# Recurrent scan gated by a SwiGLU block: B transposed on TensorE, C loaded turned last, token turns and stores on SyncE, all notices on GpSimd

## The chip, the cores and the metric

One core of one Trainium2 chip. The metric is the device time of one execution in microseconds (us); most executions of one kernel agree within about 1%, and medians are quoted with their lowest and highest. The profile is a trace of one execution.

## The reference

Cut to what matters: a layer norm, a complex diagonal recurrence over 2048 tokens, and a SwiGLU block whose output gates the result of the recurrence.

```python
# L = 2048 tokens, D = P = 448, F = 1792
xn = layernorm(x)
dt = exp(log_dt);  Lam_bar = exp(dt * Lam)
B_bar = ((Lam_bar - 1) / Lam)[:, None] * (B_re + 1j * B_im)
Bu = einsum("bld,pd->blp", xn, B_bar)
for t in range(L):                       # the scan
    h = Lam_bar * h + Bu[:, t, :]
y = 2 * einsum("blp,dp->bld", hseq, C_re + 1j * C_im).real + xn * Dskip
g = silu((silu(xn @ w_gate) * (xn @ w_up)) @ w_down)
out = x + y * g                          # bf16
```

## The kernel before

Tokens are worked in four quarters of 512. A *phase* `gu(q)` makes the gate and up products of quarter q: 14 blocks of 128 columns, two blocks to a *step*, so seven steps. `bu(q)` multiplies the tokens by B, `ssm_steps(q)` is the scan on VectorE, `down(q)` the third SwiGLU product, `out_sum(q)` the product with C. The order on TensorE is gu(0) with bu(0) inside, gu(1) with bu(1) inside, then down(0), bu(2), down(0), out_sum(0), gu(2), and so on; the tail is down(3) and out_sum(3).

D = 448 is three and a half blocks of 128. So each sum is split into two shares of half-height matmuls that run side by side, and in this program the second share of a bank starts only when the first has ended. Another engine passes that on: an empty instruction (`nop`) on that engine waits for the last matmul of the first share, and the second share waits for the `nop`. This is called a *notice*.

```python
    teller = [nc.gpsimd]

    def tell(mm):
        told = teller[0].nop(nofuse=True)            # the notice
        tc.add_manual_dep(told.ins, mm.ins.name, SYNC, reason="share")
        return told.ins.name

    def sums(banks, weights, q, c0, c1, between=None, told=None):
        for share, first in ((0, True), (1, False)):
            for n in range(len(banks)):
                ...                                  # the matmuls of this share
                        if not first and m == 0:
                            told_of(mm, left[n])     # second share waits for the notice
                if first:
                    left.append(tell(mm))
                    ...
            if first and teller[0] is nc.gpsimd:
                run_small(4)                         # four small GpSimd instructions
```

A queue of small GpSimd instructions (the parameters of the recurrence, 128x4 elements each) is emptied a few at a time *behind* each pair of notices. GpSimd works through its instructions in the order of the program, so a notice waits behind the small instructions put before it. After the fourth step of gu(0), the kernel before sends its notices on SyncE instead:

```python
    def tell_by_sync():
        teller[0] = nc.sync
        run_small(99)

    gu(0, bg, 2.0, {                     # what is issued after each step
        0: [on(table_sin, 0), on(table_phase, 2), on(table_sin, 1)],
        1: [on(b_clear), on(bu, 0, (0, 1), False), on(table_phase, 3), ...],
        2: [on(params_trig), on(bu, 0, (2,), True), *stats(6, 7), *sqrt(1)],
        3: [on(tell_by_sync), on(params_out), on(run_small, 99), *rstd_of(1),
            *norms(4, 5, 6, 7)],
        4: [on(c_weights, 0), *transposes(4, 5, 6, 7), on(ssm_steps, bg, 0)],
        ...
    }, begun)
```

SyncE also issues the loads, B and C turned (transposed by the DMA) among them; ScalarE issues the turns of the tokens and the stores of the output.

## Time and profile before

| | before |
|---|---|
| median of 3 runs | 201.40 us (201.29 to 201.56) |
| the profiled run | 204.13 us, span 202.3, mean clock 0.982 |
| first matmul of down(0) in that run | 74.55 us |
| third gate/up phase, gu(2), in that run | 97.11 to 120.59, 23.5 us |

The prediction shows the slices, TensorE's waits and the windows of the worst hole. The chain of waits: shares of the span by engine, followed back from the last instruction.

```profile
PE 46%; DVE 23%; SPq 11%; ACT 7%; DMA 7%; issue 3%; ACTq 1%; DVEq 0%
```

Only 46% of the chain runs over TensorE's own work although TensorE is busy for 92% of the span. Then GpSimd's timeline (start, duration, line, operation, out<-in with their sizes). The first line is from `params_fold`, the others are part of `params_out`:

```profile
15.60 0.32 POOL L315 TENSOR_SCALAR turn_m<-turn_m 128x12 f32<-128x12 f32 x1
...
30.06 0.49 POOL L315 TENSOR_SCALAR lam<-lam 128x4 f32<-128x4 f32 x1
30.64 0.21 POOL L315 TENSOR_TENSOR prod<-lam,pcol 128x8 f32<-128x8 f32 x1
30.93 0.20 POOL L315 TENSOR_TENSOR nb<-prod 128x4 f32<-128x4 f32 x1
```

Such a small GpSimd instruction takes 0.2 to 0.6 us in this trace, a power 1.0 to 1.1.

### The profile page before, as it was taken

What the parts mean: (1) busy time and instruction counts of PE and PEld (TensorE: products, weight loads), DVE (VectorE), ACT (ScalarE), POOL (GpSimd) and SP (SyncE); (2) the same over time, 40 slices, a digit from 0 to 9 for tenths busy, and PEclk for the clock granted to TensorE, in tenths of its full rate; (3) what the DMA queues carried; (4) which work ended last, traced back from release to release, by engine and by line L of the source; (5) the groups of instructions that cost most, each with busy time, mean ns of one, the idle gap of its engine ahead of it and who ended that gap; (6) DMA issues with size and microseconds to landing.
All of it is one profiled execution on the core that took longest, in us unless ns stands there. A gap on an engine that the chain in (4) does not pass through costs nothing.

```text
span 202.3 us, 3623 instructions
## 1 busy us (share of the span) xinstructions
PE 186.4 (92%) x1429; PEld 89.5 (44%) x1433; DVE 157.3 (78%) x243; ACT 102.7 (51%) x195; POOL 18.2 (9%) x42
## 2 busy tenths in 40 slices
PE   6786994999799999999989999999999999999990
PEld 2542431344344444455434554455444445555550
DVE  4859974097929999999989999997946889885063
ACT  2258794629798846451049755481267652402200
POOL 3374433000000200000003000000000000000000
PEclk9999999599999999999999999999999999999999
DMA  6755999990000022000110040000200000010011
GB/s 180 229 100 128 347 313 148 278 160 3 0 0 3 0 52 52 3 0 0 42 52 0 21 85 4 0 3 23 70 3 0 0 3 0 0 67 27 0 43 48
DMA packets 24648, 12.58 MB, mean 62 GB/s; under 512 B 14644, under 2 KB 24632, under 8 KB 24632
## 3 DMA queue, kind: packets, MB, share of 16 engines
q1 hardware_dynamic: 15248, 8.69, 17.5%
q10 hardware_dynamic: 9384, 3.68, 7.8%
q8 instruction: 11, 0.18, 0.3%
q14 instruction: 5, 0.04, 0.1%
HBM read 7.11 MB, written 1.84 MB: 44 GB/s over the span
## 4 chain that ended last, share of the span: by engine, by line
PE 46%; DVE 23%; SPq 11%; ACT 7%; DMA 7%; issue 3%; ACTq 1%; DVEq 0%
PE hd L563 16%; PE up L427 9%; SPq L158 9%; PE gp L427 9%; PE y L577 8%; DVE bu_im L500 3%; DMA Wu<-in_B_w_up_dram 3%; PE pb L427 3%; DVE tmp L494 3%; DVE bu_re L500 3%; DVE Vt L555 3%; DMA Wg<-in_B_w_gate_dram 2%; DVE C L390 2%; DVE ere L494 2%; ACT us L551 2%
## 5 line engine op out<-in xcount | busy, mean ns | idle before, releaser
L427 PE MATMUL up<-xT,Wu 64*128 64x512 bf16 (+1 forms) x406 | 89.0, 377 | 5.1 <-SPq L409 3.0
L427 PE MATMUL gp<-xT,Wg 64*128 64x512 bf16 (+1 forms) x406 | 90.3, 377 | 0.7 <-ACT xT L247 0.6
L550 ACT ACTIVATE gs<-gp 128x512 bf16<-128x512 f32 x56 | 34.1, 609 | 45.2 <-PE gp L427 17.6
L427 PEld LDWEIGHTS <-Wg 64*128 64x128 bf16 x406 | 37.5, 96 | 28.5 <-issue 6.3
L427 PEld LDWEIGHTS <-Wu 64*128 64x128 bf16 x406 | 37.6, 96 | 25.8 <-SPq L409 3.5
L563 PE MATMUL hd<-Wd,Vt 128*128 128x448 bf16 x224 | 43.4, 353 | 0.0
L551 ACT ACTIVATE us<-up 128x512 bf16<-128x512 f32 x56 | 34.4, 614 | 0.0
L563 PEld LDWEIGHTS <-Vt 128*128 128x128 bf16 x224 | 21.7, 98 | 21.3 <-issue 1.3
L555 DVE TENSOR_TENSOR Vt<-gs,us 128x2048 bf16<-128x2048 bf16 (+1 forms) x16 | 17.4, 1084 | 7.6 <-ACT us L551 7.6
L427 PE MATMUL pb<-xT,BT 64*128 64x512 bf16 x168 | 20.3, 376 | 3.2 <-DMA BT<-in_A_B_im_dram 1.6
L568 ACT ACTIVATE sg<-hd 128x448 bf16<-128x448 f32 x16 | 8.7, 545 | 28.2 <-PE hd L563 27.2
L590 DVE TENSOR_TENSOR t<-y,sg 128x448 f32<-128x448 f32 x16 | 10.0, 623 | 12.8 <-PE y L577 12.4
L577 PE MATMUL y<-C,H_re 128*128 128x448 bf16 x64 | 17.4, 352 | 0.0
L500 DVE TENSOR_TENSOR_SCAN bu_re<-rcol,H_re,ere 128x512 bf16<-128x512 f32 x12 | 15.1, 1268 | 0.0
L427 PEld LDWEIGHTS <-BT 64*128 64x128 bf16 x168 | 8.7, 94 | 13.9 <-issue 3.4
L225 POOL TENSOR_TENSOR sd<-vep,halves 128x1 bf16<-128x1 bf16 (+1 forms) x7 | 6.8, 970 | 84.0 <-DVE vep L220 78.3
L581 PE MATMUL y<-Dd,xT 128*128 128x128 bf16 x64 | 13.6, 212 | 0.0
L390 DVE SCALAR_TENSOR_TENSOR C<-nat,nb_im,c_tb 128x448 bf16<-128x448 bf16 (+1 forms) x4 | 2.7, 684 | 11.7 <-ACT c_tb L389 11.7
L577 PE MATMUL y<-C,H_im 128*128 128x448 bf16 x48 | 11.7, 353 | 0.0
L500 DVE TENSOR_TENSOR_SCAN bu_im<-rcol,H_im,eim 128x512 bf16<-128x512 f32 x9 | 11.4, 1261 | 0.0
L462 ACT ACTIVATE bu_re<-pb 128x512 bf16<-128x512 f32 x12 | 7.4, 614 | 7.6 <-PE pb L427 7.6
L218 DVE BATCH_NORM_STATS2 st<-x_all 128x6 f32<-128x448 bf16 x16 | 9.9, 617 | 1.6 <-DMA x_all<-in_A_x_dram 1.5
(87 smaller groups left out, 177.5 us busy)
## 6 DMA issues: line engine op xcount, KB each, us to landing
out_dram<-ob ACTq DMA_DIRECT2D x16, 112.0 KB, 1.7
Wd<-in_B_w_down_dram SPq DMA_DIRECT2D x1, 1568.0 KB, 7.6
x_all<-in_A_x_dram SPq DMA_DIRECT2D x3, 448.0 KB, 8.1
Wg<-in_B_w_gate_dram SPq DMA_DIRECT2D x3, 384.0 KB, 4.2
Wu<-in_B_w_up_dram SPq DMA_DIRECT2D x3, 384.0 KB, 5.6
Wg<-in_B_w_gate_dram SPq DMA_DIRECT2D x3, 128.0 KB, 3.4
Wu<-in_B_w_up_dram SPq DMA_DIRECT2D x3, 128.0 KB, 3.0
x_all<-in_A_x_dram SPq DMA_DIRECT2D x2, 112.0 KB
```

The costliest lines, as they stand in the source:

```text
L158: nc.sync.dma_start(out=dst[:, k, c0 : c0 + n], in_=cols, transpose=True)
L218: nc.vector.bn_stats(out=st[:], in_=x_all[:, n, :])
L427: mm = nc.tensor.matmul(banks[n][i][:, c0:c1], lhsT=weights[n][i][h, d, :], rhs=xT[h, d, q * W + c0 : q * W + c1], start=(first and m == 0 ...
L494: nc.vector.tensor_tensor(out=of(out, n), in0=of(a, n), in1=of(b, n), op=op)
L500: nc.vector.tensor_tensor_scan(out=T["b"][c][:, k, :], data0=rcol[:, k : k + 1].to_broadcast([P, W]), data1=T["e"][c][:, k, :], initial=in ...
L550: nc.scalar.activation(gs[:, i + j, :], gp_[:], ACT.Silu)
L551: nc.scalar.activation(us[:, i + j, :], up_[:], ACT.Copy)
L555: nc.vector.tensor_tensor(out=Vt[:, f0 : f0 + n, :], in0=gs[:, 0:n, :], in1=us[:, 0:n, :], op=ALU.mult)
L563: nc.tensor.matmul(hd, lhsT=Vt_of[q][:, fi, j * P : (j + 1) * P], rhs=Wd[:, fi, :], start=(fi == 0), stop=(fi == NF - 1),)
L577: nc.tensor.matmul(y, lhsT=h, rhs=C2[:, n, :], start=(n == 0), stop=(n == NS - 1))
L581: nc.tensor.matmul(y[:, s + c0 : s + P], lhsT=xT[:, n, m * P : (m + 1) * P], rhs=Dd[:, n, c0:P], start=False, stop=False,)
L590: nc.vector.tensor_tensor(out=t[:], in0=y, in1=sg[:], op=ALU.mult)
```

## The change

Its intent is to fill the holes of the first 55 us. B arrives as it lies in memory and is transposed on TensorE, beside loads that are still under way. The turned loads of C go to the end of the loads. The token turns and the output stores move from ScalarE to SyncE. Since SyncE is then busy, all notices go to GpSimd, whose small instructions now carry a cost label and are placed up to a sum of 2.0 behind each pair of notices; most carry 0.25, so that up to eight stand there instead of four. The work on C moves into gu(1), the parameters move later. The core of the diff:

```diff
-    load_turned(BT, A_B_re, 0, D)
-    load_turned(BT, A_B_im[KF * P : D, :], D, R)
-    load_turned(BT, A_B_im[0 : KF * P, :], KT * P, KF * P)
...
+    load_nat(0, A_B_re)
+    load_x(TQ, 2 * TQ)
     load_gu(C0, 768)
+    load_nat(1, A_B_im)
+    load_gu(768, F)
...
+    def b_transpose(c, d, eng):
+        tp = bank("tpb", BF16).rearrange("p (i w) -> p i w", i=2)
+        for i in range(2):
+            for k in (KF, *range(KF)):
+                ...
+                nc.tensor.transpose(tp[:, i, c0 : c0 + P], nat[:, c, k, blk(d + i)], Id[:])
+        ...                                   # one copy on ScalarE or VectorE
...
-        nc.scalar.dma_start(out=xT_of(n), in_=xn[n % TQ][:], transpose=True)
+        nc.sync.dma_start(out=xT_of(n), in_=xn[n % TQ][:], transpose=True)
...
-        told = teller[0].nop(nofuse=True)
+        told = nc.gpsimd.nop(nofuse=True)
...
-            if first and teller[0] is nc.gpsimd:
-                run_small(4)
+            if first:
+                run_small(2.0)
...
-        nc.scalar.dma_start(out=out2d[m * P : (m + 1) * P, :], in_=ob[:])
+        nc.sync.dma_start(out=out2d[m * P : (m + 1) * P, :], in_=ob[:])
...
     gu(0, bg, 2.0, {
...
+        0: [*stats(4, 5, 6, 7), *sqrt(1), on(table_phase, 0)],
+        1: [*bs(1), on(b_clear), *rstd_of(1), *norms(4, 5, 6, 7), on(table_sin, 0)],
+        2: [*transposes(4, 5, 6, 7), on(load_c), on(table_phase, 1), on(table_sin, 1),
+            on(bu, 0, (0, 1), False), on(table_phase, 2)],
+        3: [on(table_sin, 2), on(bu, 0, (2,), True), on(table_phase, 3)],
+        4: [on(table_sin, 3), on(params_trig)],
+        5: [on(params_out), on(ssm_steps, bg, 0)],
     }, begun)
```

More of the change, by code (lines that the diff above doesn't have):

```diff
@@ L134, with load_x, load_w @@
     two_pi = ctile([P, 1], F32, "two_pi")
-    def load_x(q):
+    def load_x(n0, n1):
         nc.sync.dma_start(
-            out=x_all[:, q * TQ : (q + 1) * TQ, :],
-            in_=x2d[q * W : (q + 1) * W, :].rearrange("(n p) d -> p n d", p=P),
+            out=x_all[:, n0:n1, :],
+            in_=x2d[n0 * P : n1 * P, :].rearrange("(n p) d -> p n d", p=P),
         )
-    def load_w(eng, dst, src, c0, c1):
+    def load_w(eng, eng2, dst, src, c0, c1):
         eng.dma_start(
@@ L147, in load_w, with load_nat, load_turned @@
         )
-        eng.dma_start(out=dst[:, KF, c0:c1], in_=src[blk(KF), c0:c1])
+        eng2.dma_start(out=dst[:, KF, c0:c1], in_=src[blk(KF), c0:c1])
     def load_gu(c0, c1):
-        load_w(nc.sync, Wg, B_w_gate, c0, c1)
-        load_w(nc.sync, Wu, B_w_up, c0, c1)
-    def load_turned(dst, src, c0, n):
-        for k in (slice(0, KF), slice(KF, KT)):
-            cols = src[:, 0 : KF * P] if k.start == 0 else src[:, blk(KF)]
-            nc.sync.dma_start(out=dst[:, k, c0 : c0 + n], in_=cols, transpose=True)
+        load_w(nc.sync, nc.sync, Wg, B_w_gate, c0, c1)
+        load_w(nc.sync, nc.sync, Wu, B_w_up, c0, c1)
+    def load_nat(i, src):
+        nc.sync.dma_start(
+            out=nat[:, i, 0:KF, :], in_=src[0 : KF * P, :].rearrange("(k p) f -> p k f", p=P)
+        )
+        nc.sync.dma_start(out=nat[:, i, KF, :], in_=src[blk(KF), :])
+    def load_turned(dst, src):
+        for k, cols in ((slice(0, KF), slice(0, KF * P)), (slice(KF, KT), blk(KF))):
+            nc.sync.dma_start(out=dst[:, k, :], in_=src[:, cols], transpose=True)
     nat = big.tile([P, 2, KT, D], BF16, name="nat", tag="vt")
+    natC = ctile([P, 2, KT, D], BF16, "natC")
     nc.vector.memset(Wd[:, 0, :], 0.0)
@@ L177 @@
         nc.sync.dma_start(out=x_all[:, n, :], in_=x2d[n * P : (n + 1) * P, :])
-    nc.sync.dma_start(
-        out=x_all[:, 2:TQ, :], in_=x2d[2 * P : W, :].rearrange("(n p) d -> p n d", p=P)
-    )
-    load_w(nc.scalar, Wu, B_w_up, 0, C0)
     for r, v in enumerate((A_log_dt, A_Lambda_re, A_Lambda_im, A_Dskip)):
         nc.scalar.dma_start(out=vrow[r : r + 1, :], in_=v.unsqueeze(0))
-    load_w(nc.sync, Wg, B_w_gate, 0, C0)
-    load_gu(C0, 768)
-    load_turned(BT, A_B_re, 0, D)
-    load_turned(BT, A_B_im[KF * P : D, :], D, R)
-    load_turned(BT, A_B_im[0 : KF * P, :], KT * P, KF * P)
-    load_x(1)
-    load_gu(768, 1280)
-    load_gu(1280, F)
-    load_x(2)
-    load_x(3)
-    load_turned(nat[:, 0], A_C_re, 0, D)
-    load_turned(nat[:, 1], A_C_im, 0, D)
+    load_w(nc.sync, nc.scalar, Wg, B_w_gate, 0, C0)
+    load_w(nc.sync, nc.scalar, Wu, B_w_up, 0, C0)
+    load_x(2, TQ)
+    load_nat(0, A_B_re)
+    load_x(TQ, 2 * TQ)
+    load_gu(C0, 768)
+    load_nat(1, A_B_im)
+    load_gu(768, F)
     nc.gpsimd.affine_select(
@@ L208, with gp, run_small @@
     )
+    small = deque()
+    def gp(fn, cost=0.25, **kw):
+        small.append((cost, lambda: fn(**kw)))
+    def run_small(budget):
+        while small and budget > 0:
+            cost, fn = small.popleft()
+            fn()
+            budget -= cost
     mv = ctile([P, NT, nc.vector.BN_AGGR_DIM], F32, "mv")
@@ L227, in ln_sqrt, with ln_sqrt_soon @@
         )
+    def ln_sqrt_soon(n0, n1):
+        small.appendleft((1.0, lambda: ln_sqrt(n0, n1)))
     def ln_rstd(n0, n1):
@@ L232, in ln_norm @@
     def ln_norm(n):
-        for out, cols in ((slice(0, KF * P), slice(0, KF * P)), (block(KF), blk(KF))):
+        parts = [(slice(0, D), slice(0, D))]
+        if n >= TQ:
+            parts = [(slice(0, KF * P), slice(0, KF * P)), (block(KF), blk(KF))]
+        for out, cols in parts:
             nc.vector.tensor_scalar(
@@ L244, in ln_transpose @@
         for k in range(KT):
-            nc.tensor.transpose(tp[:, k, :], xn[n % TQ][:, block(k)], Id[:])
+            nc.tensor.transpose(tp[:, k, :], xn[n][:, blk(k)], Id[:])
         if eng is nc.scalar:
@@ L278, in params_row @@
         return tv
-    def exp_of(out, in_):
-        nc.gpsimd.tensor_tensor(out=out, in0=euler[:], in1=in_, op=ALU.pow)
     def params_in():
+        g, tt = nc.gpsimd, nc.gpsimd.tensor_tensor
         are, aim = pcol[:, 0:KT, 1], pcol[:, 0:KT, 2]
-        exp_of(dtv[:], pcol[:, 0:KT, 0])
-        nc.gpsimd.tensor_tensor(out=zr[:], in0=dtv[:], in1=are, op=ALU.mult)
-        nc.gpsimd.tensor_tensor(out=zi[:], in0=dtv[:], in1=aim, op=ALU.mult)
+        gp(tt, 1.0, out=dtv[:], in0=euler[:], in1=pcol[:, 0:KT, 0], op=ALU.pow)
+        gp(tt, out=zi[:], in0=dtv[:], in1=aim, op=ALU.mult)
         for out, shift in ((thp[:], 0.0), (turn[:, 1, :], 0.25)):
-            nc.gpsimd.tensor_scalar(
-                out=out, in0=zi[:], scalar1=1.0 / (2.0 * math.pi), scalar2=shift,
-                op0=ALU.mult, op1=ALU.add,
-            )
-        exp_of(rcol[:], zr[:])
-    def fold(u, width):
-        a = work.tile([P, W], F32, name="a", tag="scr_a")[:, 0:width]
-        nc.vector.tensor_scalar(
-            out=a, in0=u, scalar1=ROUND, scalar2=ROUND, op0=ALU.add, op1=ALU.subtract
-        )
-        f = work.tile([P, W], F32, name="f", tag="scr_f")[:, 0:width]
-        nc.vector.tensor_tensor(out=f, in0=u, in1=a, op=ALU.subtract)
-        nc.vector.scalar_tensor_tensor(
-            out=a, in0=f, scalar=-1.0, in1=f, op0=ALU.mult, op1=ALU.max
-        )
-        return f, a
+            gp(g.tensor_scalar, out=out, in0=zi[:], scalar1=1.0 / (2.0 * math.pi),
+               scalar2=shift, op0=ALU.mult, op1=ALU.add)
+        gp(tt, out=zr[:], in0=dtv[:], in1=are, op=ALU.mult)
+        gp(tt, 1.0, out=rcol[:], in0=euler[:], in1=zr[:], op=ALU.pow)
     def cos_sin(c_out, s_out, f, a, sign):
@@ L309, in cos_sin @@
         nc.scalar.activation(c_out, a, ACT.Sin, scale=-TWO_PI, bias=half_pi[:])
-    small = deque()
-    def gp(fn, **kw):
-        small.append(lambda: fn(**kw))
-    def run_small(n):
-        while small and n:
-            small.popleft()()
-            n -= 1
     def wide(name):
@@ L343, in params_fold @@
         for k in range(KT):
-            gp(g.tensor_scalar, out=Dd[:, k, :], in0=Id[:], scalar1=pcol[:, k + k // KF, 3:4],
+            gp(g.tensor_scalar, 0.6, out=Dd[:, k, :], in0=Id[:], scalar1=pcol[:, k + k // KF, 3:4],
                scalar2=1.0, op0=ALU.mult, op1=ALU.mult)
@@ L370, in table_phase @@
     def table_phase(k):
-        u = work.tile([P, W], F32, name="u", bufs=1)
-        nc.vector.tensor_single_scalar(u[:], it_f[:], thp[:, k : k + 1], ALU.mult)
-        phase[k] = fold(u[:], W)
+        f = work.tile([P, W], F32, name="f", tag="scr_f")
+        a = work.tile([P, W], F32, name="a", tag="scr_a")
+        nc.vector.tensor_single_scalar(f[:], it_f[:], thp[:, k : k + 1], ALU.mult)
+        nc.vector.tensor_scalar(
+            out=a[:], in0=f[:], scalar1=ROUND, scalar2=ROUND, op0=ALU.add, op1=ALU.subtract
+        )
+        nc.vector.tensor_tensor(out=f[:], in0=f[:], in1=a[:], op=ALU.subtract)
+        nc.vector.scalar_tensor_tensor(
+            out=a[:], in0=f[:], scalar=-1.0, in1=f[:], op0=ALU.mult, op1=ALU.max
+        )
+        phase[k] = f[:], a[:]
     def table_sin(k):
         cos_sin(CT[:, k, :], ST[:, k, :], *phase.pop(k), two_pi[:] if k == KF else TWO_PI)
+    def b_transpose(c, d, eng):
+        tp = bank("tpb", BF16).rearrange("p (i w) -> p i w", i=2)
+        for i in range(2):
+            for k in (KF, *range(KF)):
+                c0 = blk(k).start if c == 0 else (k + 1) % KT * P
+                nc.tensor.transpose(
+                    tp[:, i, c0 : c0 + P], nat[:, c, k, blk(d + i)], Id[:]
+                )
+        tp = tp[:, :, c * R : c * R + D]
+        dst = BT[:, d : d + 2, c * D : (c + 1) * D]
+        if eng is nc.scalar:
+            nc.scalar.activation(dst, tp, ACT.Copy)
+        else:
+            nc.vector.tensor_copy(out=dst, in_=tp)
     def b_clear():
@@ L388, in c_weights @@
             tb = work.tile([P, W], F32, name="c_tb", tag="scr_" + "fa"[i])[h, 0:D]
-            nc.scalar.activation(tb, nat[h, 1, k, :], ACT.Copy, scale=v[h, k : k + 1])
+            nc.scalar.activation(tb, natC[h, 1, k, :], ACT.Copy, scale=v[h, k : k + 1])
             nc.vector.scalar_tensor_tensor(
-                out=C2[ho, o, :], in0=nat[h, 0, k, :], scalar=u[h, k : k + 1], in1=tb,
+                out=C2[ho, o, :], in0=natC[h, 0, k, :], scalar=u[h, k : k + 1], in1=tb,
                 op0=ALU.mult, op1=ALU.subtract,
@@ L403 @@
     SYNC = mybir.DependencyInfo(mybir.DependencyClass.Sync, mybir.DependencyReason.DATA)
-    teller = [nc.gpsimd]
     def tell(mm):
-        told = teller[0].nop(nofuse=True)
+        told = nc.gpsimd.nop(nofuse=True)
         tc.add_manual_dep(told.ins, mm.ins.name, SYNC, reason="share")
@@ L592, in finish @@
         nc.vector.tensor_tensor(out=ob[:], in0=t[:], in1=x_all[:, m, :], op=ALU.add)
-        nc.scalar.dma_start(out=out2d[m * P : (m + 1) * P, :], in_=ob[:])
+        nc.sync.dma_start(out=out2d[m * P : (m + 1) * P, :], in_=ob[:])
     bg = Background()
-    def tell_by_sync():
-        teller[0] = nc.sync
-        run_small(99)
     def on(fn, *args):
@@ L611 @@
         ln_transpose(n, nc.scalar)
-        warm(1 + 2 * n)
+        if n == 0:
+            warm(1)
+    nc.scalar.activation(pcol[:], params_row(), ACT.Copy)
+    warm(1)
     for n in range(2, TQ):
@@ L620 @@
         ln_norm(n)
-    ln_transpose(2, nc.scalar)
+    ln_transpose(2, nc.vector)
     ln_transpose(3, nc.vector)
-    nc.scalar.activation(pcol[:], params_row(), ACT.Copy)
     params_in()
     params_fold()
+    for d in range(0, KT, 2):
+        b_transpose(0, d, nc.scalar)
     gu_matmuls(0, 0, begun, W // 2, W)
     nc.sync.dma_start(out=Wd[:], in_=B_w_down.rearrange("(ft p) d -> p ft d", p=P))
-    table_phase(0)
-    table_phase(1)
+    load_x(2 * TQ, NT)
     bu_alloc(0)
@@ L641, in sqrt, with bs, load_c @@
     def sqrt(q):
-        return [on(ln_sqrt, q * TQ, (q + 1) * TQ)]
+        return [on(ln_sqrt_soon, q * TQ, (q + 1) * TQ)]
     def rstd_of(q):
         return [on(ln_rstd, q * TQ, (q + 1) * TQ)]
-    gu(0, bg, 2.0, {
-        0: [on(table_sin, 0), on(table_phase, 2), on(table_sin, 1)],
-        1: [on(b_clear), on(bu, 0, (0, 1), False), on(table_phase, 3), on(table_sin, 2),
-            on(table_sin, 3), *stats(4, 5)],
-        2: [on(params_trig), on(bu, 0, (2,), True), *stats(6, 7), *sqrt(1)],
-        3: [on(tell_by_sync), on(params_out), on(run_small, 99), *rstd_of(1),
-            *norms(4, 5, 6, 7)],
-        4: [on(c_weights, 0), *transposes(4, 5, 6, 7), on(ssm_steps, bg, 0)],
-        5: [on(c_weights, 1)],
-        6: [on(c_weights, 2)],
+    def bs(c):
+        return [on(b_transpose, c, d, nc.vector if d else nc.scalar) for d in range(0, KT, 2)]
+    def load_c():
+        load_turned(natC[:, 0], A_C_re)
+        load_turned(natC[:, 1], A_C_im)
+    gu(0, bg, 2.0, {
+        0: [*stats(4, 5, 6, 7), *sqrt(1), on(table_phase, 0)],
[5 more added lines that the diff above has]
+        5: [on(params_out), on(ssm_steps, bg, 0)],
     }, begun)
     bu_alloc(1)
-    gu(1, bg, 2.0, {
-        0: [on(bu, 1, (0, 1, 2), True), on(c_weights, 3)],
+    gu(1, bg, 1.7, {
+        0: [on(bu, 1, (0, 1, 2), True)],
         1: [*stats(8, 9), on(ssm_steps, bg, 1)],
-        2: stats(10, 11) + sqrt(2),
-        3: rstd_of(2) + norms(8, 9),
-        4: norms(10, 11),
-        5: transposes(8, 9),
-        6: transposes(10, 11),
+        2: [*stats(10, 11), *sqrt(2), on(run_small, 99), on(c_weights, 0)],
+        3: [*rstd_of(2), *norms(8, 9), on(c_weights, 1)],
+        4: [*norms(10, 11), *transposes(8, 9), on(c_weights, 2)],
+        5: [*transposes(10, 11), on(c_weights, 3)],
     })
@@ L688 @@
                 2: rstd_of(q + 3) + norms(n, n + 1),
-                3: norms(n + 2, n + 3),
-                4: transposes(n, n + 1),
-                5: transposes(n + 2, n + 3),
+                3: norms(n + 2, n + 3) + transposes(n, n + 1),
+                4: transposes(n + 2, n + 3),
             } if q + 3 < NQ else {})
```

## The prediction

> **What bounds the kernel now.** TensorE does. I read the 40 slices first, then TensorE's waits, then the windows and timelines around each wait.
>
> ```profile
> PE   6786994999799999999989999999999999999990
> DVE  4859974097929999999989999997946889885063
> ACT  2258794629798846451049755481267652402200
> PEclk9999999599999999999999999999999999999999
> ```
>
> A slice is 5.06 us. After slice 10 (about 55 us) TensorE is full nearly everywhere; what it loses lies in the first 55 us. The clock row has one 5, just after the slice with TensorE at 4. VectorE is empty in that slice and full from 60 us on, so it may become a rival. TensorE's waits name the holes:
>
> ```profile
> PE up L427 <- SPq L409: 3.0, 1, 3.0
> PE pb L427 <- DMA BT<-in_A_B_im_dram: 1.6, 1, 1.6
> PE pb L427 <- ACT gs L550: 1.4, 1, 1.4
> PE up L427 <- POOLq L409: 1.1, 2, 0.8
> PE up L427 <- DVE t L590: 0.8, 1, 0.8
> ```
>
> The largest is a notice: the second half of each sum waits for a semaphore that SyncE passes on (line 409). SyncE itself was held by the loads of C with transposition, as its timeline shows:
>
> ```profile
> 25.88 5.30 SPq L158 DMA_TRANSPOSE nat<-in_A_C_re_dram  x2
> 31.22 3.48 SPq L158 DMA_TRANSPOSE nat<-in_A_C_im_dram  x2
> 34.83 0.50 SPq L627 DMA_DIRECT2D Wd<-in_B_w_down_dram  x1
> ```
>
> The notice follows at 35.45, behind these three in SyncE's order. The windows give its second price: busy times of the five engines, then clock, DMA share and GB/s.
>
> ```profile
> 32.00:35.50 3.50, 0.49 (x8) 0.06 (x4) 1.23 (x1) 0.69 (x2) 0.21 (x2) 0.86 1.30 149
> 35.50:41.00 5.50, 5.50 (x28) 1.91 (x30) 1.03 (x2) 3.29 (x6) 0.00 (x0) 0.50 0.96 288
> ```
>
> For 5.5 us after the hole the granted clock is 0.50: 13 pairs of half-height matmuls start 0.425 us apart instead of 0.215, so 13 x 0.21 = 2.7 us more are lost. Last, ScalarE's timeline at the start of the third gate/up phase:
>
> ```profile
> 98.57 5.02 ACTq L593 DMA_DIRECT2D out_dram<-ob  x4
> 103.69 0.60 ACT L550 ACTIVATE gs<-gp 128x512 bf16<-128x512 f32 x1 [12.02 <-DVE ob L592]
> ```
>
> ScalarE stands 12 us behind its four stores, which wait for VectorE, while the PSUM banks of the gate/up step that ended near 100.1 us wait for it.
>
> **What the Trainium skill says.** "TensorE: Matmul & The Clock Gate", Part 1, has the array drop to half clock after an idle window of about 3.4 us and come back after a busy one. The trace agrees in kind: a hole of 3.0 us was enough, and half clock lasted 5.5 us. So filling that hole is worth nearly twice its length. The same page, Part 4, gives about 275 to 390 ns for one 128x128 transposition; here eight in a row took 0.83 us, 0.10 each, and I use that. "DMA: Bandwidth & Descriptors", Issuing engines are not separate DMA queues, says that another issuing engine saves only sequencer time. That is the point of the moved stores and turns: a turn holds its queue for about 1.25 us here, a plain transfer 0.35 to 0.5. "ScalarE: Activation LUTs", What ACT_TABLE_LOAD costs, gives 186 ns + 0.833 ns per element with immediate operands: 0.61 us for 512, where the trace has 0.60. I estimate the new 896-wide PSUM copies at 0.93 us from it.
>
> **The change, part by part.** I count on TensorE. A gate/up step of two blocks is 14 pairs x 0.215 = 3.0 us; a bu step of two blocks 3.0, of one block with the packed bank 2.4, of three with it 5.35.
>
> *Loads.* B arrives untransposed, so the turned loads that held SyncE from 7.8 to 17.6 us go. The built program shows every DMA waiting for the one eight places before it. By that rotation the last 64 rows of the first columns of Wg and Wu, now on ScalarE's queue, go out after the first Wu block and after the next ScalarE slot: about 5.3 and 5.8 us. Similar 64 KB pieces took 3.6 to 3.8 us to land, but there was more ahead of them, so I say 8.2 and 8.7. The first matmuls can start at about 7.4 (7.92 before; one norm instruction instead of two, ScalarE not stuck issuing), but the fourth row group waits until 8.7. The first half then ends at 9.9, against 9.45. Bytes ahead of Wu columns 256 to 768 are about 2.8 MB; at the 250 GB/s of the first microseconds from 2 us on they land near 13.1, just in time. Columns 768 on, another 2.6 MB with B_im, land near 23, needed at 24 to 27.
>
> *Transposes of B.* 32 at 0.083 to 0.10 us are about 3.0 us of new TensorE work, half before the second half of step 0, half after step 1. The copies, three on ScalarE and one on VectorE, lie beside it.
>
> *Timetable.* First half ends 9.9; tokens 2 and 3 turned, 10.7; B_re, 12.2; second half (1.5 us), 13.7 (before 13.4). Step 1, 16.7; B_im, 18.2; step 2, 21.2; bu(0), 24.2; step 3, 27.2; bu(0) rest, 29.6; steps 4 to 6, 38.6. Phase 1: step 0, 41.6; bu(1), 47.0; six steps, 65.0. In the trace of before phase 1 ended, and the first down matmul began, at 74.55. That is 9.6 us. Read as removed terms after 13.4 us: notices and issue gaps 0.9, B's DMA and gap 1.8, SyncE's notice 3.2, clock 2.7, bu(1)'s wait for ScalarE and its ragged restart 2.2, crumbs 0.2, sum 11.0; less B_im 1.5 and 0.3 at the start, 9.2. The two ways differ by 0.4; I take 9.3.
>
> *Notices on GpSimd.* A notice for the first block has 0.85 us to spare. The batches of small work cost up to 2.0 by their labels, but eight light operations such as copies and turn_m sum to about 3.2 us in the trace of before. One notice should come late by about 0.5 us: 8.8 left.
>
> *Stores on SyncE.* ScalarE can empty the banks of the third phase's first step at once. That phase took 23.4 us (97.1 to 120.5) against 21.0 of work. What stays is the second step waiting for y banks that VectorE frees late, about 0.8. Gain 1.6. The other phases and the tail (down, y, last store) don't change.
>
> Sum: 8.8 + 1.6 = 10.4; 201.4 - 10.4 = **191.0 us**.
>
> **Rivals.** *VectorE becomes the bound.* It is 95 to 98% busy from 60 to 140 us, and TensorE now arrives nine us earlier. For it: no slack in those slices, and the work on C (about 4.7 us) moves into the second phase. Against it: VectorE sits idle 6.7 us in 32 to 41 and 5.7 us in 41 to 60, and this is where the new order puts work. Placing its new order against my timetable, H of the first quarter is ready near 75.5 and wanted at 81; the first y is read 4.4 us late, against 5.0 before. If I am wrong by 3 us, the third phase waits longer: about 194.
>
> *The loads come late.* With 7.9 MB before the token turns in one queue, at 280 GB/s the turns land at 31 to 35 us and are wanted at 38.6. The step-1 weights have no margin. A hole of 1 to 3 us, and half clock if it nears 3 us, gives 193 to 197.
>
> *The wait was hidden anyway.* If SyncE's hole only handed over to another wait (tokens turned at 38.7 to 44.2 in before), half the gain stays: 196. Against it: after, the turns go out from about 19 us, not behind ScalarE's evictions.
>
> **Range and chances.** My sum 191.0; nothing lost at the start and no late notice makes it 188.5; one rival at its middle makes 194 to 195. Range 188 to 195.5. Only two rivals together, or a second half-clock stretch, bring it over 197.4: faster by over 2% 0.92, within 2% 0.07, slower 0.01.
>
> **What would show it.** Right: no clock dip near 35 us; no TensorE wait over 1 us between 14 and 60 us; no BT DMA in TensorE's waits; 32 new transposes of about 3 us in sum; the first down matmul near 65.5 us; ScalarE's 12 us wait before gs gone, and the third phase 22 us long. Wrong: a wait for Wg, Wu or xT DMA above 2 us, a clock of 0.5 after 10 us, GpSimd notices above 1.5 us in sum, or TensorE waiting for H or for y banks by more than 3 us.

## The result, and the profile after

| | before | after |
|---|---|---|
| median | 201.34 us, 4 runs (201.25 to 201.56) | 198.51 us, 4 runs (197.36 to 198.69) |
| ratio | | 0.9846 (95%: 0.9808 to 0.9884) |
| profiled run | 204.13 us, span 202.3, clock 0.982 | 198.54 us, span 196.8, clock 0.991 |
| first matmul of down(0) | 74.55 | 71.33 |
| gu(2) | 23.5 us | 21.7 us |

A ratio is the mean time of one kernel's fast runs over that of the other's of the same rounds, so it is not quite the ratio of the medians. 191.0 us had been predicted, with a range of 188 to 195.5. The slices after (40 of 4.92 us, tenths of busy time):

```profile
PE   7899799949999999999999999999999999999991
DVE  4698982499228999999899999998945799789263
POOL 3335940195002000000003000000000000000000
PEclk9999999996999999999999999999999999999999
```

After 55 us the rows look as hoped. But TensorE has a 4 again (39 to 44 us), with a clock of 6 in the next slice, and GpSimd, which had nothing to do at that time in the kernel before, shows a 9 in just that slice (and another at 20 to 25 us). TensorE's waits (engine, operation, line, what it waited for; sum in us, times, longest):

```profile
PE up L440 <- POOLq L422: 3.0, 1, 3.0
PE pb L440 <- POOLq L422: 1.3, 1, 1.3
PE warm L176 <- DVE Wd L167: 1.1, 1, 1.1
PE gp L440 <- DMA Wg<-in_B_w_gate_dram: 0.5, 1, 0.5
```

The waits for SyncE, for B's DMA, for ScalarE and for the output banks are gone. Two waits for notices on GpSimd (line 422) have come in, one of them 3.0 us long. (The wait for `Wd` is the start of the program, before and after alike.) The windows around it (busy time of TensorE, weight loads, VectorE, ScalarE, GpSimd with counts, then clock, DMA share, GB/s):

```profile
38.00:41.60 3.60, 3.56 (x34) 1.41 (x30) 3.57 (x5) 3.00 (x6) 2.62 (x4) 1.00 0.02 5
41.60:44.60 3.00, 0.01 (x2) 0.01 (x2) 2.97 (x4) 0.00 (x0) 2.84 (x4) 0.92 0.00 0
44.60:48.00 3.40, 3.40 (x20) 1.25 (x22) 3.37 (x5) 1.72 (x4) 2.56 (x3) 0.57 0.01 2
```

TensorE stands from 41.6 to 44.6 us, and for 3.4 us after that the clock averages 0.57, which costs another 3.4 x 0.43 = 1.5 us. No transfer is under way; VectorE and GpSimd are both busy for the whole hole. GpSimd's timeline shows what stands in front of the notice:

```profile
38.73 0.61 POOL L212 TENSOR_TENSOR lam<-lam,rcol 128x12 f32<-128x12 f32 x1 [11.77 <-PE up L440]
39.44 1.20 POOL L212 TENSOR_SCALAR lam<-lam 128x4 f32<-128x4 f32 x1
40.72 0.75 POOL L212 TENSOR_TENSOR prod<-lam,pcol 128x8 f32<-128x8 f32 x1
41.55 1.06 POOL L212 TENSOR_TENSOR nb<-prod 128x4 f32<-128x4 f32 x1
42.69 0.80 POOL L212 TENSOR_TENSOR prod<-lam,pcol 128x8 f32<-128x8 f32 x1
43.56 0.91 POOL L212 TENSOR_TENSOR nb<-prod 128x4 f32<-128x4 f32 x1
44.43 0.64 POOL L212 TENSOR_TENSOR b_re<-nb,rden 128x4 f32<-128x4 f32 x1
45.03 1.11 POOL L212 TENSOR_TENSOR b_im<-nb,rden 128x4 f32<-128x4 f32 x1
```

These are the instructions that took 0.2 to 0.5 us before. Now they take 0.6 to 1.2 us. VectorE's timeline of the same microseconds says why:

```profile
38.07 1.22 DVE L507 TENSOR_TENSOR tmp<-bu_im,ST 128x2048 bf16<-128x2048 bf16 x1
39.32 1.23 DVE L507 TENSOR_TENSOR ere<-ere,tmp 128x2048 bf16<-128x2048 bf16 x1
40.46 0.95 DVE L507 TENSOR_TENSOR eim<-bu_im,CT 128x1536 bf16<-128x1536 bf16 x1
41.33 1.23 DVE L568 TENSOR_TENSOR Vt<-gs,us 128x2048 bf16<-128x2048 bf16 x1
42.48 0.94 DVE L507 TENSOR_TENSOR tmp<-bu_re,ST 128x1536 bf16<-128x1536 bf16 x1
43.46 0.96 DVE L507 TENSOR_TENSOR eim<-eim,tmp 128x1536 bf16<-128x1536 bf16 x1
```

Read the two lists side by side. `ere` ends at 39.32 + 1.23 = 40.55, and GpSimd's `lam`, begun during it, at 40.64. `eim` ends at 41.41, `prod` at 41.47; `Vt` at 42.56, `nb` at 42.61; `tmp` at 43.42, `prod` at 43.49; `eim` at 44.42, `nb` at 44.47. Each small GpSimd instruction ends 0.05 to 0.1 us after the VectorE instruction that was running when it began, whatever its own size. Each of these six needs the result of the one before, so the next one begins just after VectorE has begun its next, and loses most of a VectorE instruction again. TensorE resumes at 44.59, after the `nb` that ended at 44.47.

Eight instructions stand in front of the notice, `b_re` and `b_im` too, and these two end only at 45.07 and 46.14. So this notice did not wait until everything before it had ended: it went once `b_im`, the last before it, had its input, that `nb`.

The Trainium skill has this. "SBUF — State Buffer", Who interferes with whom, says that "A DVE instruction with two SBUF inputs contends with a GpSimd instruction that reads SBUF", since VectorE's second input comes through the read port that the two engines share, and that the later of the two is blocked until the first has ended. All six VectorE instructions above take two SBUF inputs, and the trace agrees to within 0.1 us. The prediction does not name this page.

The second wait, 1.3 us before `pb` at 22.43, is of the same kind: on GpSimd's timeline

```profile
20.70 1.63 POOL L212 TENSOR_SCALAR turn_m<-turn_m 128x12 f32<-128x12 f32 x1
```

took 1.63 us where it took 0.32 before. It began beside a VectorE product (`Vt`, 20.68, 1.21 us) and ended at 22.33, just after VectorE's next instruction (`f<-it_f,thp`, 21.82, 0.47 us), so it seems to have lost two. The second of them has one tensor input and a column of scalars, so the sentence quoted does not cover it. TensorE resumes at 23.69, when the last small instruction in front of this notice (`den`, 23.66) has just begun.

What the change meant to do otherwise worked. The transposes of B on TensorE's timeline:

```profile
10.53 1.06 PE L383 MATMUL tpb<-Id,nat 128*128 128x128 bf16 x16
16.50 1.07 PE L383 MATMUL tpb<-Id,nat 128*128 128x128 bf16 x16
```

32 transposes took 2.13 us, against an estimate of 3.0.

### The profile page after: what moved, and what is told of

It reads as the page before. It is cut to its first block, busy times and chain, and to the rows that moved or that the text cites. A ratio compares the mean times of both kernels' runs of the same rounds, so it can differ in the third digit from the quotient of the medians.

```text
span 196.8 us, 3681 instructions
## 1 busy us (share of the span) xinstructions
PE 186.6 (95%) x1463; PEld 90.6 (46%) x1463; DVE 157.8 (80%) x241; ACT 104.9 (53%) x197; POOL 25.7 (13%) x42
## 4 chain that ended last, share of the span: by engine, by line
PE 88%; POOL 5%; DMA 3%; issue 1%; DVE 1%; SPq 1%; POOLq 0%; DVEq 0%
PE gp L440 23%; PE hd L576 22%; PE up L440 19%; PE y L590 11%; PE pb L440 9%; PE pk L463 2%; DMA Wg<-in_B_w_gate_dram 2%; PE y L594 2%; DMA Wu<-in_B_w_up_dram 2%; POOL turn_m L212 1%; POOL nb L212 1%; PE tpb L383 1%; POOL lam L212 1%; POOL prod L212 1%; POOL turn L212 0%
## 5 line engine op out<-in xcount | busy, mean ns | idle before, releaser
L440 PE MATMUL up<-xT,Wu 64*128 64x512 bf16 (+1 forms) x406 | 87.4, 373 | 3.0 <-POOLq L422 3.0
L440 PE MATMUL gp<-xT,Wg 64*128 64x512 bf16 (+1 forms) x406 | 88.4, 373 | 0.5 <-DMA Wg<-in_B_w_gate_dram 0.5
L440 PEld LDWEIGHTS <-Wu 64*128 64x128 bf16 x406 | 36.9, 95 | 24.0 <-POOLq L422 4.0
L576 PEld LDWEIGHTS <-Vt 128*128 128x128 bf16 x224 | 21.7, 98 | 21.3 <-issue 1.3
L440 PE MATMUL pb<-xT,BT 64*128 64x512 bf16 x168 | 19.5, 379 | 1.3 <-POOLq L422 1.3
L590 PE MATMUL y<-C,H_re 128*128 128x448 bf16 x64 | 17.4, 352 | 0.0
L440 PEld LDWEIGHTS <-BT 64*128 64x128 bf16 x168 | 8.0, 95 | 12.4 <-issue 2.0
L590 PE MATMUL y<-C,H_im 128*128 128x448 bf16 x48 | 11.7, 353 | 0.0
L605 DVE TENSOR_TENSOR ob<-t,x_all 128x448 bf16<-128x448 f32 x16 | 10.0, 624 | 0.6
```

Source lines behind the costliest of these rows:

```text
L440: mm = nc.tensor.matmul(banks[n][i][:, c0:c1], lhsT=weights[n][i][h, d, :], rhs=xT[h, d, q * W + c0 : q * W + c1], start=(first and m == 0 ...
L576: nc.tensor.matmul(hd, lhsT=Vt_of[q][:, fi, j * P : (j + 1) * P], rhs=Wd[:, fi, :], start=(fi == 0), stop=(fi == NF - 1),)
L590: nc.tensor.matmul(y, lhsT=h, rhs=C2[:, n, :], start=(n == 0), stop=(n == NS - 1))
L605: nc.vector.tensor_tensor(out=ob[:], in0=t[:], in1=x_all[:, m, :], op=ALU.add)
```

## The experiments

Twelve runs were made, two of them of the unchanged kernels, on three chips, and each is compared with runs of the kernel before on its own chip. The theory: *VectorE's two-input products stretch the small GpSimd instructions, and the notice behind them is late.* Rivals: the start or the clock is at fault; SyncE or the loads; the number or order of the GpSimd instructions as such; the wait merely uncovers another one.

### Notices by SyncE over the critical stretch

```diff
+    teller = [nc.gpsimd]
-        told = nc.gpsimd.nop(nofuse=True)
+        told = teller[0].nop(nofuse=True)
...
-        5: [on(params_out), on(ssm_steps, bg, 0)],
+        5: [on(params_out), on(tell_by, nc.sync), on(ssm_steps, bg, 0)],
...
-        1: [*stats(8, 9), on(ssm_steps, bg, 1)],
+        1: [on(tell_by, nc.gpsimd), *stats(8, 9), on(ssm_steps, bg, 1)],
```

> The changed kernel, with the notices given by SyncE instead of GpSimd for the last gate/up step of phase 0, the first of phase 1 and bu(1) only; nothing else moves. Theory A (a notice stands behind eight small GpSimd instructions that are stretched beside VectorE's bf16 work): the hole of 3.0 us near 41.6 us and the half clock after it go, the small instructions stay slow (lam to nb_im about 8 us in sum), time 198.5 - 3.0 - 1.2 = 194.3 us. Theory B (TensorE would have waited there for PSUM banks or for ScalarE anyhow): a hole of 2 to 3 us stays, with another releaser, time 197.5 to 198.5.

Measured: 194.84 us (193.90 to 195.21, 4 runs), ratio 0.9647 (0.9582 to 0.9712). The 3.0 us hole and the low clock behind it are gone, and the first matmul of down(0) moves from 71.33 to 67.89 us, although this profile has a low clock (0.50 from 8.7 to 12.0 us) that the one of the kernel after does not have. The small instructions are as slow as in the kernel after:

```profile
39.50 1.08 POOL L212 TENSOR_SCALAR lam<-lam 128x4 f32<-128x4 f32 x1
40.67 1.14 POOL L212 TENSOR_TENSOR prod<-lam,pcol 128x8 f32<-128x8 f32 x1
```

So it is not their slowness as such that costs, but that a notice stands behind them. Taking the notice out of that queue brings most of the loss back. The 1.3 us wait before `pb`, where the notices stayed on GpSimd, is still there.

### The parameters one step earlier

```diff
-        3: [on(table_sin, 2), on(bu, 0, (2,), True), on(table_phase, 3)],
-        4: [on(table_sin, 3), on(params_trig)],
-        5: [on(params_out), on(ssm_steps, bg, 0)],
+        3: [on(table_sin, 2), on(bu, 0, (2,), True), on(table_phase, 3), on(params_trig)],
+        4: [on(table_sin, 3), on(params_out)],
+        5: [on(ssm_steps, bg, 0)],
```

> The changed kernel, with the sine of the parameters one step earlier and the nine small GpSimd instructions that follow it one step earlier, in 33 to 37 us, where VectorE stands idle; same instructions, same number, notices still by GpSimd. Theory A (VectorE's work stretches them): the nine take about 2.5 to 3.5 us instead of 8, the hole is below 0.7 us, time about 194.5 us. Theory C (it is only their number and order before the notice): the hole stays near 3 us, merely a step earlier, time 198 us.

Measured: 194.43 us, the median of the three fast runs (194.10 to 195.47; 194.95 with the slow one), ratio 0.9654 (0.9587 to 0.9721, fast runs). The profiled run, 197.09 us, was slow in its first 15 us and is not used for times; its timelines of GpSimd,

```profile
39.46 0.21 POOL L212 TENSOR_TENSOR prod<-lam,pcol 128x8 f32<-128x8 f32 x1
39.74 0.20 POOL L212 TENSOR_TENSOR nb<-prod 128x4 f32<-128x4 f32 x1
40.02 0.20 POOL L212 TENSOR_TENSOR prod<-lam,pcol 128x8 f32<-128x8 f32 x1
40.30 1.14 POOL L212 TENSOR_TENSOR nb<-prod 128x4 f32<-128x4 f32 x1
```

and of VectorE

```profile
40.15 1.23 DVE L507 TENSOR_TENSOR ere<-bu_re,CT 128x2048 bf16<-128x2048 bf16 x1 [6.13 <-ACT CT L310]
```

show the switch: the same instruction, `nb`, takes 0.20 us while VectorE is idle and 1.14 us once `ere` has begun. The number and order of the GpSimd instructions are those of the kernel after, so number and order alone are refuted.

### The scan one step later

```diff
-        5: [on(params_out), on(ssm_steps, bg, 0)],
+        5: [on(params_out)],
...
-        0: [on(bu, 1, (0, 1, 2), True)],
+        0: [on(bu, 1, (0, 1, 2), True), on(ssm_steps, bg, 0)],
```

> The changed kernel, with VectorE's scan work of the first quarter begun one step later and GpSimd left as it is: the other way round to keep the two apart. Theory A: the nine small instructions take 3 to 4 us, only the Vt product of VectorE lying beside them, the hole is below 1 us; VectorE gets 4 us later, which may cost up to 2 us at the first y banks: 194.5 to 196.5 us. Theory C: hole stays 3 us, 198 to 200 us.

Measured: 197.20 us (196.26 to 198.53), ratio 0.9785 (0.9717 to 0.9853), not resolved against 2%, and above the 194.5 to 196.5 expected. Nothing about GpSimd was edited, yet

```profile
38.77 0.21 POOL L212 TENSOR_TENSOR lam<-lam,rcol 128x12 f32<-128x12 f32 x1 [11.76 <-PE up L440]
39.07 1.27 POOL L212 TENSOR_SCALAR lam<-lam 128x4 f32<-128x4 f32 x1
40.43 0.20 POOL L212 TENSOR_TENSOR prod<-lam,pcol 128x8 f32<-128x8 f32 x1
```

of the six from the first `lam` to the second `nb` all are short but the one that began beside the only VectorE product there (`Vt`, 39.02 to 40.25). The last three, from 41.43 on, lie beside VectorE's next instructions and take 0.69 to 1.18 us; `b_im` ends at 43.26, and TensorE works through from 41 to 44 us all the same. The hole is gone and down(0) begins at 66.89 us. But VectorE is now late with the last quarter's scan, and TensorE waits for it at 181.8 us:

```profile
PE y L590 <- DVE H_re L507: 2.2, 1, 2.2
```

So the mechanism is confirmed from the other side, and VectorE's slack at the end is shown to be small: this order of work gives back 2.2 us of what it gains.

### The kernel before with its notices on GpSimd

```diff
-        3: [on(tell_by_sync), on(params_out), on(run_small, 99), *rstd_of(1),
+        3: [on(params_out), on(run_small, 99), *rstd_of(1),
...
-        1: [*stats(8, 9), on(ssm_steps, bg, 1)],
+        1: [on(tell_by_sync), *stats(8, 9), on(ssm_steps, bg, 1)],
```

> The kernel before, with one part of the change: the notices stay on GpSimd until the second step of phase 1, so that none stands behind SyncE's turned loads of C. If SyncE's order alone made the 3.0 us hole of the kernel before (my prediction's first term), it goes and the time falls by 3 us, to 198.3; if ScalarE's scaling of C, which needs the same loads, takes its place (rival: the wait was hidden anyhow), ScalarE stops at c_tb until about 38.5 us, TensorE stops for PSUM banks a step later, and the time is 200 to 201.5.

Measured: 201.74 us (201.29 to 202.91), ratio 1.0014 (0.9954 to 1.0074). The SyncE wait is gone, and in its place stands

```profile
PE gp L427 <- DMA xT<-xn: 4.3, 1, 4.3
```

TensorE waits for the turned tokens of the next quarter until 43.74 us. ScalarE issues their four turns from 35.57 to 41.39 us here and from 35.74 to 41.42 in the usual run of the kernel before (shown in the section "The kernel before, once more"), so the earlier notice did not bring them forward. That run stands twice, 1.7 us for SyncE and 2.2 us until 43.54; this one stands once, 4.3 us, and ends the wait at the same time. So in the kernel before the notices alone are worth nothing that these runs can measure: a second wait stood behind. That ScalarE's place as issuer held the turns back is argued; no run moved the turns alone. The expectation named another second wait, for ScalarE's scaling of C; it did not come.

### The kernel after again, and with four more warm-up matmuls

The first is the unchanged kernel, for comparison. The second adds fillers while the first weights arrive:

```diff
         if n == 0:
-            warm(1)
+            warm(2)
     nc.scalar.activation(pcol[:], params_row(), ACT.Copy)
-    warm(1)
+    warm(4)
```

> The changed kernel unchanged, on the chip and in the rounds of the three that follow, to compare them with. Expected 198.3 us, 197.3 where the profile shows no stretch of half clock; hole of 3.0 us near 41.6 us.

> The changed kernel with four more filler matmuls before its first gate/up step (2 and 4 instead of 1 and 1), where TensorE otherwise waits for the last rows of Wg and Wu until about 8.4 us. Two profiles of the last call showed half clock between 8 and 15 us, costing up to 2.8 us. Theory A [...]: no half clock before 20 us in the profile, time 0.3 to 1 us below the changed kernel's, with less spread. Theory B (the early half clock has another cause, or is rare): same time within 0.3 us.

Measured: 199.66 us (198.53 to 200.47), ratio 0.9848 (0.9771 to 0.9925), and 199.38 us (198.92 to 200.56), ratio 0.9847 (0.9775 to 0.9919). The same holes, 3.0 and 1.3 us, and the same low clock behind the first stand in the repeat. The fillers made no difference. Neither of these two profiles has a low clock in its first 15 us, so whether they protect a run that has one stays open.

### Stores by ScalarE again

```diff
-        nc.sync.dma_start(out=out2d[m * P : (m + 1) * P, :], in_=ob[:])
+        nc.scalar.dma_start(out=out2d[m * P : (m + 1) * P, :], in_=ob[:])
```

> The changed kernel with its 16 stores issued by ScalarE again. Theory (my prediction's 1.6 us): ScalarE waits about 12 us behind its stores at the start of phase 2, the third gate/up phase takes 23.4 us instead of 21.7, time 1.6 us above the changed kernel's, 199.9. Rival (VectorE's late release of the y banks sets that phase's start anyhow): under 0.5 us of difference.

Measured: 200.01 us (199.09 to 200.74), ratio 0.9881 (0.9802 to 0.9960), so 0.35 us over the repeat by medians, with ranges that overlap. ScalarE again stands behind its stores,

```profile
94.77 4.60 ACTq L606 DMA_DIRECT2D out_dram<-ob  x4
99.42 0.60 ACT L563 ACTIVATE gs<-gp 128x512 bf16<-128x512 f32 x1 [10.73 <-PE up L440]
```

but TensorE has no hole there, and gu(2) takes 21.8 us, as long as with the stores on SyncE (21.7). So the move of the stores is not what shortened gu(2) from 23.5 us. What differs from before is when VectorE is through: it reads the first output bank at 93.1 us in the kernel after, before gu(2) begins at 93.7, against 97.3 for a phase that begins at 97.1 in the kernel before. TensorE's waits say the same: in gu(2) of the kernel before it waits 0.8 us for VectorE's `t` (`PE up L427 <- DVE t L590` in the prediction's list), the instruction that reads an output bank, and in the kernel after that wait is gone. An earlier VectorE as the cause fits these times and was not tested by itself.

### B turned by the DMA, the rest of the change kept

```diff
-    load_nat(0, A_B_re)          # natural load + 16 TensorE transposes
+    load_bt(0)                   # turned load straight into BT
-    load_nat(1, A_B_im)
+    load_bt(1)
-    for d in range(0, KT, 2):
-        b_transpose(0, d, nc.scalar)
```

(names shortened; the B_im transposes go too.)

> The changed kernel with B loaded turned by DMA again, at the places where it now loads B untransposed; the 32 transposes on TensorE and their copies go. Theory A (turned loads hold SyncE about 1.25 us each and delay all weights behind them): TensorE saves 2.1 us of transposes and waits 3 to 5 us more for Wg, Wu or BT in its first 25 us, time 199.5 to 202. Theory B (queue room was enough, and B on TensorE costs its 2.1 us for nothing): about 196.3.

Measured: 199.00 us (197.49 to 200.29), ratio 0.9817 (0.9730 to 0.9904), which is not resolved from the repeat's 0.9848. My theory, that B's turned loads would hold up the weights by 3 to 5 us, is wrong: no wait for B stands in TensorE's list. But the rival's 196.3, the whole 2.1 us saved, did not come either. This run's profile has six waits of 0.2 to 0.7 us, 2.3 us together, in its first 14 us, where the kernel after has one of 0.5 (the start, `Wd`, left out in both); it also has a low clock from 8.5 to 18.5 us, so its times say little. The TensorE transposes cost 2.1 us and bring nothing that these runs can measure.

### Three versions put together

The first has the earlier parameters, the fillers, and half the room for small GpSimd instructions behind each pair of notices between step 2 and the last sine of gu(0):

```diff
-                run_small(2.0)
+                run_small(room[0])       # 2.0, but 1.0 from step 2 to table_sin(3)
```

The second is the first with B turned by the DMA. The third is the first with the last sine, the parameters and the first scan another step earlier:

```diff
-        3: [on(table_sin, 2), on(bu, 0, (2,), True), on(table_phase, 3), on(params_trig)],
-        4: [on(table_sin, 3), on(set_room, 2.0), on(params_out)],
-        5: [on(ssm_steps, bg, 0)],
+        3: [on(table_sin, 2), on(bu, 0, (2,), True), on(table_phase, 3), on(table_sin, 3),
+            on(set_room, 2.0), on(params_out)],
+        4: [on(ssm_steps, bg, 0)],
```

with `params_trig` moved to the end of step 2.

> e2_trig_early, with the batch of small GpSimd work after one sum halved between the second gate/up step and the sine of the parameters (four light instructions instead of eight ahead of the next notice), and the extra fillers of w_warm. Theory A: the 1.3 us hole near 22 us goes as well, TensorE waits for no GpSimd notice over 0.3 us: 193.4 us where the changed kernel gives 198.5, ratio to the kernel before 0.960. If that 1.3 us hole only hands over to another wait (ScalarE's copies of B, say): 194.7.

> b1_combo with B loaded turned by DMA (as in e6). If the turned loads of B cost TensorE no wait once the notices are right, it saves the 2.1 us of transposes: 191.5 us, ratio 0.95. If B on TensorE pays for itself by letting the weights come earlier: 193 to 195 us.

> b1_combo with the sine, the nine small instructions and VectorE's first scans one more gate/up step earlier. VectorE's idle 6 us before its first scans shrinks to 3; if that helps where VectorE sets the end (first y banks, H), 0.5 to 1 us below b1_combo; if TensorE is bound by its own work everywhere, the same within 0.3 us; if the nine instructions then meet VectorE's tables, a notice comes 1 us late again.

| | median, us (lowest to highest of 6) | ratio (95%) | first down(0) |
|---|---|---|---|
| put together | 193.19 (192.68 to 193.92) | 0.9549 (0.9514 to 0.9585) | 66.28 |
| same, B turned by the DMA | 192.65 (192.00 to 193.01) | 0.9525 (0.9489 to 0.9561) | 64.83 |
| same, one step earlier | 192.26 (192.01 to 193.75) | 0.9519 (0.9479 to 0.9559) | 65.16 |

The second came out between its two expectations (191.5, and 193 to 195). The three are not resolved from each other; all beat both kernels: the one before by 4.5 to 4.8%, the one after by about 3% (0.952 over the repeat's 0.985). The slices of the third, GpSimd and the clock included:

```profile
PE   7999999999999999999999999999999999999991
POOL 3235763200020000000030000000000000000000
PEclk9999999999999999999999999999999999999997
```

No slice of TensorE after the first is below 9 until the last one. The chain of the same run is 97% TensorE. No wait for a notice is left, the 1.3 us one included, although `turn_m` still takes 1.63 us at 20.61 in it: with half the room there is less in front of the notice. With the fillers alone and with the earlier parameters alone the 1.3 us wait stayed, so it is the halved room that took it away. Eight of the nine parameter instructions run from 31.15 to 33.12 us at 0.20 to 0.24 us each, while VectorE is idle; the ninth, behind the next pair of notices, takes 1.13 us beside `ere`.

### The kernel before, once more

> The kernel before, once more with a profile. Its first profiled run took 204.1 us, 2.7 above its median, and had 5.5 us of half clock behind the 3.0 us hole. If the half clock is what sets that run apart, a profile of a run near 201.4 us shows the hole without half clock (or with a short stretch), and 2.7 us of my prediction's sum weren't in the time to be beaten. If the half clock is always there, this run is also near 204, or the stretch is there at 201.4.

Measured: 201.63 us, span 199.8, clock 0.991, close to the medians. The profile of this usual run differs from the one that the prediction was worked from. TensorE's waits,

```profile
PE gp L427 <- ACT us L551: 2.2, 1, 2.2
PE up L427 <- SPq L409: 1.7, 1, 1.7
PE pb L427 <- DMA BT<-in_A_B_im_dram: 1.2, 1, 1.2
```

and the windows after the two larger holes:

```profile
33.80:41.30 7.50, 7.50 (x68) 3.22 (x68) 3.89 (x5) 3.17 (x6) 0.00 (x0) 1.00 1.11 274
...
43.60:49.00 5.40, 5.40 (x36) 2.13 (x38) 4.85 (x7) 4.59 (x9) 0.00 (x0) 0.69 0.02 3
```

The hole at SyncE's notice is 1.7 us and the clock stays at 1.00 behind it; the low clock comes later and milder (5.4 x 0.31 = 1.7 us against 2.7). The first matmul of down(0) stands at 72.06 us, not at 74.55.

## Why the prediction was wrong

The prediction was a gain of 10.4 us. Against the usual run of before, at the same clock of 0.991, the span fell from 199.8 to 196.8, by 3.0. By stretches:

| stretch | predicted gain | measured gain |
|---|---|---|
| up to the first matmul of down(0) | 8.8 | 72.06 - 71.33 = 0.7 |
| gu(2) | 1.6 | 23.46 - 21.69 = 1.8 |
| everything else | 0 | 0.5 |
| sum | 10.4 | 3.0 |

So the whole error, 7.4 us, lies in the first stretch, which fell short by 8.1. Two steps failed there: the cost of the small instructions in front of the notices, and the trace that the gain was subtracted from.

**"Notices on GpSimd. ... One notice should come late by about 0.5 us: 8.8 left."** This step failed. It took each small instruction at its duration in the trace of before, 0.2 to 0.6 us, although the change puts them beside VectorE's two-input products, where they took 0.6 to 1.6. The one late notice that it foresaw, behind the copies and `turn_m`, came 1.3 us late; the one of 3.0 us, behind the parameters, is not in its sum. Two notices came late, by 3.0 and 1.3 us, and the low clock behind the first cost 1.5: 5.8 us instead of 0.5. For the 3.0 us notice the cause is shown three ways: notices taken off GpSimd (0.9647), the GpSimd work moved to where VectorE is idle (0.9654), and VectorE's work moved away without touching GpSimd (the hole went). For the 1.3 us one the runs show that the number of instructions in front of it decides; that VectorE stretched `turn_m` is read from one trace. The prediction also carried its own warning: it noted that the first loss doubles through the clock, and kept "a second half-clock stretch" for its worst case, but did not apply it to a notice of its own.

**"In the trace of before phase 1 ended, and the first down matmul began, at 74.55. That is 9.6 us."** The base of the subtraction was wrong by 74.55 - 72.06 = 2.5 us. The profiled run had taken 204.13 us, 2.7 more than the median of 201.40 from which I subtracted. Both numbers were there to see. (The 25 runs of the kernel before in the later calls show mean clocks of 0.985 to 1.000; that run had 0.982.) The removed terms "SyncE's notice 3.2, clock 2.7" were sizes of that one longer run; the usual run has 1.7 and 1.7.

The two make 5.3 + 2.5 = 7.8 of the 8.1. Since the transposes were 0.9 us cheaper than estimated, about 1.2 us is left in smaller losses that I did not break down.

What held:

- **Timetable.** It put the first matmul of down(0) near 65.5 us. The kernel without late notices (the third of those put together) has it at 65.16 and takes 192.26 us. The working of TensorE's stream was right to within a microsecond for a kernel whose notices are on time. In part that is luck: the transposes cost 0.9 us less than estimated, so something else costs more.
- **Loads.** In the kernel after the largest wait for weights was 0.5 us; the B wait is gone; token turns and C are in time. The rival "the loads come late" did not happen there; in two later profiles (earlier parameters, first of those put together) TensorE waited 1.3 us for Wu, so "no margin" was right.
- **VectorE as the bound** did not happen in the kernel after. The late scan shows how near it is: 2.2 us.
- **"The wait was hidden anyway"** was the right picture for the kernel before (its notices alone: 1.0014), and wrong for the change, which moves the turns too.
- **Third phase.** 21.7 us measured for 22 predicted, but the reason given failed, so the number is luck: with the stores back on ScalarE it is 21.8. The 0.8 us for the output banks, which it said would stay, is what went.
- **Transposes.** 2.13 us, not 3.0. The copies on ScalarE took 0.95 us alone, against the 0.93 estimated.

What would prove it wrong was named in the text, and it is what happened: "a clock of 0.5 after 10 us" and "GpSimd notices above 1.5 us in sum".

Of the low clock after the hole one thing stays open: one of the four runs of the kernel after shows a mean clock of 1.000 and took 197.36 us, the others 0.987 to 0.991 and 198.5 to 198.7. The same hole is followed by a low clock in some runs and, it seems, not in all; no trace of such a run was taken.

## What to carry to other kernels

An instruction that only passes a signal on waits behind the work put before it on its engine, here until the last instruction before it had its inputs: give it a queue without work, or count that work at the duration it has beside its new neighbours, above all GpSimd instructions beside VectorE instructions with two SBUF inputs. Before subtracting from a median what a trace shows, compare the profiled run's own time with that median. When a hole is closed in parts, check with an experiment which second wait stands behind the first.

## What the Trainium skill lacked or had wrong

- "SBUF — State Buffer", Who interferes with whom: the rule is right, and these runs agree (a 128x4 parameter instruction took 0.20 to 0.49 us in the trace of before and 0.64 to 1.20 us in that of after, the six of the hole ending within 0.1 us of VectorE's). It does not say that a chain of dependent small GpSimd instructions loses to a back-to-back VectorE stream at every link: the six from 38.73 to 44.47 us took 5.7 us, against 1.7 us for the same six while VectorE was idle (31.15 to 32.81 in the third of those put together). Nor does that page follow this on to a `nop` used as a signal behind them: 3.0 us of TensorE.
- "TensorE: Matmul & The Clock Gate", Part 4: its 275 to 390 ns are for one 128x128 transposition (0.22 us in this trace) and are not what a stream costs; 16 in a row took 1.06 us, 0.066 us each.
- "TensorE: Matmul & The Clock Gate", Part 1: it gives one idle window of about 3.4 us as what brings half clock. Here shorter holes were enough, so the window need not be idle throughout: a hole of 3.0 us was followed by a mean clock of 0.57 for 3.4 us, and one of 2.2 us by 0.69 for 5.4 us, while the 1.7 us hole ten us before that was followed by 1.00.
